# Order of the opening transfers, of the first feed-forward steps and of PE's instructions in an attention and feed-forward kernel

## The chip, the cores and the metric

The kernel runs on 1 core of one Trainium2 chip. The metric is device time in microseconds (us) of one execution. A core has five engines with a queue each: PE (matmuls and transposes), DVE and ACT (elementwise work and reductions), POOL (here only constants at the start) and SP, which issues all the DMA transfers of this kernel.

## The reference

Three stages in float32 (weights arrive as float64 and are converted on the chip):

```
attention: q, k, v are (2 batches, 8 heads, 768 positions, 64)
  k_sum = max of k over blocks of 32,  v_sum = mean of v over blocks of 32   (24 blocks)
  scores = q.k / 8 where |i - j| < 16 (else -1e9), beside q.k_sum / 8 + log(32)
  out = softmax(scores over both parts) @ [v, v_sum]
x = out as (1536 tokens, 512)
x = relu(x @ w_in)^2 @ w_out                         (d_ff 2048)
x = x / rms(x) * g;  out = (silu(x @ w_gate) * (x @ w_val)) @ w_out2   (d_ff 1536)
```

## The kernel before

**Attention** goes by groups of 128 queries of all 8 heads: 12 groups, 6 per batch. For a batch, `prep_load` loads the keys in three chunks, `prep_k` transposes a chunk on PE, takes the block maxima on DVE and copies the transposed keys to `kT` on ACT, and `prep_kend` puts the maxima between them. `vm_load` and `vmean` make the block means of the values (tile `vm`, evacuated by ACT at L383), and `vmfix` copies them by four small transfers per call into the tile `vx`, next to the value rows that `vload(g)` (six transfers, L404) puts there for a group. `vx` holds two groups at a time. A group is then `qload`/`qprep` (queries of two groups: load, transpose, scale), `scores` (PE, L418), `softmax` (DVE and ACT), `ptrans` (transposes on PE, copies to `pT` on ACT, L468), and `av` (PE, L488, needs `pT` and `vx`), whose result `split_xs` parts into a high and a low half `xhi`, `xlo`. `softmax` has two ways of taking the exponential: with `EXPACT(g)` true eight activations on ACT, one per head, that also sum; otherwise one long activation, with the subtraction and the sum as two more passes on DVE (L452, L454).

**Feed-forward 1** goes in three rounds over d_ff (4, 6 and 6 blocks of 128: `ROUNDS1`). The first round is woven into the attention: the loop over `k_` (six steps) takes two groups of tokens per step, with `h_pair(k_, f)` (x @ w_in, 24 matmuls of 128x256) and `y_pair(k_, f)` (12 matmuls of 128x512 into `y`) for f = 0 and 2, and between them the attention of the groups `g = 2 k_ + 3` and `g + 1`. Rounds 2 and 3 and feed-forward 2 follow, a stream of dense matmuls. Every product is three matmuls (high x high, high x low, low x high).

**Weights** come as 512 KB tiles of raw float64 (L160 for `wi`, L164 for `wo`). The class `Units` takes them in the list `order` (`wi0..3`, `wo0..3`, then those of round 2, ...) through four stages: `load`, `conv_a` (two activations on ACT, L175 and L176), `conv_b` (four passes on DVE, L182 to L189) and `split` (ACT L195, DVE L196). `tick()` moves one tile on by one stage in each of them; `until(u)` ticks until `u` is ready; `TICKS` extra ticks stand at the end of a step of the first round. `cap` holds loads to eight tiles until the third step. Raw tiles, converted tiles and the loaded keys, queries and value chunks share one tag of 14 tiles (`NW`).

**What sets the order.** The kernel text gives a program order. When it is compiled, a scheduler walks a modelled timeline and puts on each engine's queue what is ready first there, earlier program order winning; so each engine's order, SP's too, can differ from the text. Waits between the engines are added after that. `tc.manual_schedule` holds the engines that it names to program order. `tc.issue_after`, wrapped by `after(mark)`, puts all that is issued in its block behind the marked instruction on the same engine's queue, without waiting for its end.

**The opening of the text before:** keys of batch 0, queries 0, weight tiles `wi0`, `wi1` (`E0`), queries of the groups 2 and 3, values, weight tiles up to the sixth (`E1`), `prep_k`, scores 0, row loads `vload(0)` and `vload(1)`, scores 1, `vmean`, `vmfix`, and then groups 2, 3 and 4 with `av(0)` to `av(2)`; the loop over `k_` begins with the keys of batch 1.

Of the kernel before, what the change touches and what calls it, by code (L numbers as in the profile page):

```python
# [32 lines left out]
def tile_window_attention_moe_moe2(  # L33
# [13 lines left out]
    nc = tc.nc  # L47
# [19 lines left out]
    NG = NT // P  # L67
    NC2 = GPB // 2
# [164 lines left out]
                self.tick()  # L233

    def EXPACT(g):
        return g < 2 or g % 2 == 1

    def PARTS(g):
        return 2 if g < 3 else 1

    QB = 2
    E0, E1, TICKS = 2, 6, 2
    WARM = 10
    WOLAG = 2
    order = [("wi", f) for f in range(ROUNDS1[0])] + [("wo", f) for f in range(ROUNDS1[0])]
# [9 lines left out]
    units1 = Units(order)  # L255
# [18 lines left out]
    mark = {}  # L274
# [34 lines left out]
    def prep_begin(b):  # L309
        ksum = ap_.tile([P, NPAIR, NB], F32, tag="ksum", name=f"ksum{b}", bufs=1)  # L310
        state[b] = ksum
# [28 lines left out]
    def prep_kend(b, a):  # L340
        ksum = state[b]
        gaps = kT[:, :, WIN : WIN + NW1 * STEP].rearrange("d p (n s) -> d p n s", s=2 * STEP)
        half = ksum[:, :, GAP * a : GAP * (a + 1)]
        nc.vector.tensor_copy(
            gaps[:, :, :, STEP * a : STEP * a + GAP],
            half.unsqueeze(2).to_broadcast([P, NPAIR, NW1 // 2, GAP]),
        )
        if a == 0:
            nc.vector.tensor_copy(kT[:, :, WIN + NW1 * STEP : WIN + NW1 * STEP + GAP], half)
# [4 lines left out]
    def qload(g):  # L354
        b, r = divmod(g, GPB)
        state[("q", g)] = token_chunk(q, b, r // 2, f"qr{g}")
# [30 lines left out]
    def vmfix(i0, n):  # L387

        vt = vx.rearrange("k (i u) h d -> k u i (h d)", u=2)
        for u in range(2):  # L390
            for j, a in ((WIN, u), (K0 + QT, 1 - u)):
                rows = state["vm"][GAP * a : GAP * (a + 1)]
                nc.sync.dma_start(  # L393
                    vt[j : j + GAP, u, i0 : i0 + n], rows.unsqueeze(1).to_broadcast([GAP, n, DM])
                )

    def vload(g):
        b, r = divmod(g, GPB)
        i0 = 2 * g % NVX
        for u in range(2):  # L400
            t0 = r * P + u * QT
            for j, n, o in ((0, WIN, t0 - WIN), (K0, QT, t0), (K1, WIN, t0 + QT)):
                o = min(max(o, 0), S - n)
                nc.sync.dma_start(  # L404
                    vx[j : j + n, i0 + u], v[b, :, o : o + n, :].rearrange("h s d -> s h d")
                )
# [19 lines left out]
    def softmax(g):  # L426
        r = g % GPB
        mk = masks["first" if r == 0 else ("last" if r == GPB - 1 else "mid")]
        sl = state.pop(("s", g))
        te = ap_.tile([P, 2, NPAIR, NK], F32, tag="t", name=f"t{g}", bufs=TB)  # L430
        t = te.rearrange("q e p n -> q (e p) n")
        state[("t", g)] = t
        mx = ap_.tile([P, H], F32, tag="mx", name=f"mx{g}", bufs=TB)
        sm = ap_.tile([P, H], F32, tag="sm", name=f"sm{g}", bufs=TB)
        parts = PARTS(g)
        n = H // parts
        for i in range(parts):
            hs = slice(n * i, n * i + n)
            tv, m_, s_ = t[:, hs], mx[:, hs], sm[:, hs]
            for e in range(2 // parts * i, 2 // parts * (i + 1)):  # L440
                nc.vector.tensor_tensor(  # L441
                    te[:, e], sl[e], mk.unsqueeze(1).to_broadcast([P, NPAIR, NK]), op=ALU.add
                )
            if EXPACT(g):
                nc.vector.reduce_max(m_, tv, axis=AX.X, negate=True)
                for h in range(hs.start, hs.stop):
                    mark[("exp", g)] = nc.scalar.activation(
                        t[:, h], t[:, h], AF.Exp, bias=mx[:, h : h + 1], accum_out=sm[:, h : h + 1]
                    )
            else:  # L450
                nc.vector.reduce_max(m_, tv, axis=AX.X)
                nc.vector.tensor_tensor(tv, tv, m_.unsqueeze(2).to_broadcast([P, n, NK]), op=ALU.subtract)  # L452
                mark[("exp", g)] = nc.scalar.activation(tv, tv, AF.Exp)
                nc.vector.reduce_sum(s_, tv, axis=AX.X)  # L454
            nc.vector.tensor_scalar_add(s_, s_, 1e-9)
            nc.vector.reciprocal(s_, s_)
            mark[("norm", g)] = nc.vector.tensor_tensor(
                tv, tv, s_.unsqueeze(2).to_broadcast([P, n, NK]), op=ALU.mult
            )
# [21 lines left out]
    def av(g):  # L481
        pT = state.pop(("pT", g))
        ps = psA(f"xps1_{g}")
        for u in range(2):
            for p in range(NPAIR):
                o = p * P + QT * u
                for e in range(2):
                    nc.tensor.matmul(  # L488
                        ps[QT * e : QT * e + QT, o : o + QT],
                        vx[:, (2 * g + u) % NVX, 2 * p + e, :],  # L490
                        pT[:, e * NPAIR + p, QT * u : QT * u + QT],
                        start=True, stop=True,
                    )
        split_xs(ps, g, 1)
        state["done"] = g
# [85 lines left out]
    def group(g):  # L581

        scores(g)
        if g > 3:
            vload(g)
        softmax(g)
        if g + 2 < NG and g % 2 == 0:
            qload(g + 2)


    wz = cpool.tile([P, P], F32, name="wz")
    nc.vector.memset(wz, 0.0)
    nc.scalar.activation(ss[:, 0:1], wz[:, 0:1], AF.Exp)
# [4 lines left out]
    for c in range(NC2):  # L598
        prep_load(0, c)
    qload(0)  # L600
    units1.load(E0)
    qload(2)
    for c in range(NC2):
        vm_load(0, c)
    units1.load(E1)
    for j in (0, LK - WIN):
        nc.gpsimd.memset(kT[:, :, j : j + WIN], 0.0)
    prep_k(0, 0)
# [4 lines left out]
    qprep(0)  # L613
    prep_kend(0, 1)
    scores(0)
    vload(0)
    vload(1)
    softmax(0)
    scores(1)
    for c in range(NC2):  # L620
        vmean(0, c)
    vmfix(0, NVX // 2)
    softmax(1)
    rot["tags"] = ("a", "x")
    units1.ahead = 3
    qprep(2)
    ptrans(0)
    group(2)
# [5 lines left out]
    vload(3)  # L634
    ptrans(2)
    qprep(4)
    av(2)
    group(4)


    def steps_of(rounds, firsts):
# [31 lines left out]
        t = square(ps, f"0_{k_}_{f}")  # L673
        hq[(k_, f)] = hsplit(t, CH, f"0_{k_}_{f}")

    def y_pair(k_, f):
        if f == 0:
            for m in range(2):
                ys[m] = y_tile(k_, m, "y0_")
        hh = hq.pop((k_, f))  # L680
        for j in range(2):
            units1.until(("wo", f + j))
            ff_out(
                [ys[m] for m in range(2)], [t[:, G2 * j : G2 * (j + 1)] for t in hh],
                W[("wo", f + j)], f + j == 0, f + j == ROUNDS1[0] - 1,
            )
        if k_ == NK2 - 1:
            units1.used += 4
        if f == ROUNDS1[0] - 2:
            for m in range(2):  # L690
                gather(2 * k_ + m, ys.pop(m), 0, ROUNDS1, "y", None)

    def keys(b):
        prep_begin(b)
        for c in range(NC2):
            prep_k(b, c)
        prep_kend(b, 0)
        prep_kend(b, 1)

    for k_ in range(NK2):
        g, last = 2 * k_ + 3, 2 * k_ + 3 >= NG
        if k_ == 0:
            for c in range(NC2):
                prep_load(1, c)
        h_pair(k_, 0)
        if not last:
            ptrans(g)
        if g == GPB - 1:  # L710
            group(GPB)
        h_pair(k_, 2)
        if not last:
            av(g)
        if g == GPB - 1:
            for c in range(NC2):
                vmean(1, c)
            vmfix(0, 1)
        if g + 2 < NG:
            group(g + 2)  # L720
            if g + 2 == GPB + 1:
                vmfix(1, 1)
        y_pair(k_, 0)
        if g + 1 < NG:
            ptrans(g + 1)
        if k_ == 0:
            keys(1)
            for c in range(NC2):
                vm_load(1, c)
        elif g + 3 < NG:  # L730
            qprep(g + 3)
        y_pair(k_, 2)
        if g + 1 < NG:
            av(g + 1)
        if k_ == 0:
            qprep(GPB)
        elif g + 3 < NG:
            group(g + 3)
        if k_ == 2:
            units1.cap = NW - 3  # L740
        for _ in range(TICKS):
            units1.tick()
        if not last and g == NG - 1:
            actx.close()
            rot["tags"] = ("a",)
            side["pool"] = ctx.enter_context(
                tc.tile_pool(name="w2pool", bufs=1, side="right", reuse_waits="tile")
            )
            side["psum"] = ctx.enter_context(
                tc.tile_pool(name="psY2", bufs=1, space=PSUM, reuse_waits="tile")  # L750
            )
            grow = side["pool"].tile([P, DM], F32, tag="grow", name="grow")
            nc.sync.dma_start(grow, rms_g.partition_broadcast(P))
            units1.cap = NW + NRIGHT - 3

    steps1 = [s_ for s_ in steps_of(ROUNDS1, FIRST1) if s_[0] > 0]
    n1 = len(steps1)
    for i in range(n1 + 2):
# [97 lines left out]
```

## Time and profile before

| what | value |
|---|---|
| median of 3 runs (lowest, highest) | 694.28 us (691.59, 694.9) |
| the profiled execution | 692.37 us, its span 690.7 us |
| PE busy | 655.9 us, 95% of the span |
| DVE, ACT, POOL busy | 409.0, 300.6, 4.1 us |
| mean granted clock of PE | 0.97 of full |
| bytes read from HBM | 50.07 MB |
| transfers under 512 B a packet | 46080 of 78188 packets |

The span runs from the first to the last instruction; what the profiled execution has beyond it (1.7 us) lies outside. The shares are averages over the whole span, and the kernel has stages with different limits, so they don't say what bounds a stage. A clock of 1.00 is 2.4 GHz, 0.50 is 1.2 GHz. Idle time of PE is listed in the profile with the event that ended it.

### The profile page before, as it was taken

To read this page: it belongs to the slowest core of one execution; us is meant where nothing else is said; L and a number is where in the kernel's file an instruction comes from. 1 tells how busy PE (TensorE), PEld (TensorE's weight loads), DVE (VectorE), ACT (ScalarE), POOL (GpSimd) and SP (SyncE) were. 2 spreads that over 40 slices of the span, in tenths; PEclk is the share of its full clock that TensorE was granted. 3 is DMA by queue.
4 is the path that set the end of the run, shared out by engine and by line. 5 is a ranking of instruction groups with operands and counts; after the bars stand their busy time and mean duration, and the time that the engine had idled before them with its cause. 6 is when DMAs were issued, how large, how long until landed. Compare 5 with 4: busy or idle time off the path is not lost.

```text
span 690.7 us, 9362 instructions
## 1 busy us (share of the span) xinstructions
PE 655.9 (95%) x3644; PEld 532.7 (77%) x3644; DVE 409.0 (59%) x737; ACT 300.6 (44%) x607; POOL 4.1 (1%) x25
## 2 busy tenths in 40 slices
PE   6838998799999999999999999999999999999997
PEld 5337867688888888888888888888888888888885
DVE  4976858784999838924856596269933131313132
ACT  4835646655675526525453664257621121111110
POOL 2000000000000000000000000000000000000000
PEclk9758999899999999999999999999999999999999
DMA  9994244341722222101023043014300000001011
GB/s 232 276 236 115 47 115 121 94 126 26 248 88 85 81 79 93 61 1 49 13 70 113 31 143 101 1 61 123 121 1 1 0 1 0 1 0 62 1 61 62
DMA packets 78188, 54.22 MB, mean 79 GB/s; under 512 B 46080, under 2 KB 72704, under 8 KB 78144
## 3 DMA queue, kind: packets, MB, share of 16 engines
q1 hardware_dynamic: 78144, 53.62, 26.7%
q8 instruction: 29, 0.48, 0.3%
q14 instruction: 15, 0.12, 0.1%
HBM read 50.07 MB, written 3.15 MB: 77 GB/s over the span
## 4 chain that ended last, share of the span: by engine, by line
PE 84%; DVE 6%; DMA 4%; SPq 3%; ACT 2%; issue 1%; DVEq 0%; ACTq 0%
PE h L509 19%; PE y L530 18%; PE g L509 14%; PE v L509 14%; PE z L530 14%; DMA raw_wi<-in_moe_w_in_dram 2%; PE xps L488 2%; DMA raw_wo<-in_moe_w_out_dram 1%; PE s L418 1%; SPq L404 1%; DVE t L441 1%; SPq L303 1%; PE xps L500 1%; SPq L393 1%; DMA vx<-in_v_dram 1%
## 5 line engine op out<-in xcount | busy, mean ns | idle before, releaser
L509 PE MATMUL h<-xhi,w_wi 128*128 128x512 f32 (+1 forms) x480 | 132.8, 350 | 2.1 <-DMA vx<-in_v_dram 2.1
L530 PE MATMUL y<-w_wo,hhi 128*128 128x512 f32 x384 | 121.3, 399 | 0.0
L802 DVE TENSOR_TENSOR sg<-v,sg 128x512 f32<-128x512 f32 x36 | 24.8, 690 | 134.8 <-PE v L509 134.8
L509 PEld LDWEIGHTS h<-xhi,w_wi 128*128 128x128 f32 x480 | 84.8, 189 | 15.0 <-ACT xhi L478 2.3
L509 PE MATMUL v<-xhi,w_wv 128*128 128x512 f32 x288 | 95.5, 392 | 0.0
L509 PE MATMUL g<-xhi,w_wg 128*128 128x512 f32 x288 | 95.3, 392 | 0.0
L530 PE MATMUL z<-w_wp,hhiz 128*128 128x512 f32 x288 | 89.3, 393 | 0.0
L509 PE MATMUL h<-xlo,w_wi 128*128 128x512 f32 (+1 forms) x240 | 83.8, 350 | 0.9 <-DVE xlo L479 0.9
L530 PEld LDWEIGHTS y<-w_wo,hhi 128*128 128x128 f32 x384 | 71.8, 189 | 16.0 <-ACT u_wi L176 0.3
L530 PE MATMUL y<-w_wo,hlo 128*128 128x512 f32 x192 | 74.8, 395 | 0.0
L800 ACT ACTIVATE sg<-g 128x512 f32<-128x512 f32 x36 | 21.5, 598 | 103.9 <-PE g L509 101.6
L509 PEld LDWEIGHTS g<-xhi,w_wg 128*128 128x128 f32 x288 | 54.0, 188 | 12.3
L509 PEld LDWEIGHTS v<-xhi,w_wv 128*128 128x128 f32 x288 | 54.0, 188 | 12.1
L530 PEld LDWEIGHTS z<-w_wp,hhiz 128*128 128x128 f32 x288 | 54.0, 188 | 12.1
L658 ACT ACTIVATE r<-h 128x512 f32<-128x512 f32 x48 | 28.7, 598 | 69.8 <-PE h L509 69.7
L509 PE MATMUL g<-xlo,w_wg 128*128 128x512 f32 x144 | 56.6, 393 | 0.0
L509 PE MATMUL v<-xlo,w_wv 128*128 128x512 f32 x144 | 56.5, 392 | 0.0
L530 PE MATMUL z<-w_wp,hloz 128*128 128x512 f32 x144 | 56.0, 393 | 0.0
L659 DVE TENSOR_TENSOR r<-h,r 128x512 f32<-128x512 f32 x48 | 33.0, 687 | 36.3 <-ACT r L658 35.9
L520 ACT CAST hhiz<-sg 128x512 fp32r<-128x512 f32 x36 | 22.3, 620 | 70.6 <-DVE sg L802 70.3
L509 PEld LDWEIGHTS h<-xlo,w_wi 128*128 128x128 f32 x240 | 45.4, 189 | 7.4 <-DVE xlo L479 1.1
L530 PEld LDWEIGHTS y<-w_wo,hlo 128*128 128x128 f32 x192 | 35.8, 188 | 8.1
(125 smaller groups left out, 900.5 us busy)
## 6 DMA issues: line engine op xcount, KB each, us to landing
raw_wi<-in_moe_w_in_dram SPq DMA_DIRECT2D x16, 512.0 KB
raw_wo<-in_moe_w_out_dram SPq DMA_DIRECT2D x16, 512.0 KB
raw_wg<-in_moe_w_gate_dram SPq DMA_DIRECT2D x12, 512.0 KB
raw_wv<-in_moe_w_val_dram SPq DMA_DIRECT2D x12, 512.0 KB
raw_wp<-in_moe_w_out_dram SPq DMA_DIRECT2D x12, 512.0 KB
kr<-in_k_dram SPq DMA_DIRECT2D x12, 256.0 KB
qr<-in_q_dram SPq DMA_DIRECT2D x12, 256.0 KB
vr<-in_v_dram SPq DMA_DIRECT2D x6, 512.0 KB
```

The source lines that it names most:

```text
L303: nc.sync.dma_start(t[:, j].rearrange("p (h d) -> p h d", h=H), src[b, :, o : o + P, :].rearrange("h p d -> p h d"),)
L393: nc.sync.dma_start(vt[j : j + GAP, u, i0 : i0 + n], rows.unsqueeze(1).to_broadcast([GAP, n, DM]))
L404: nc.sync.dma_start(vx[j : j + n, i0 + u], v[b, :, o : o + n, :].rearrange("h s d -> s h d"))
L418: mark[("s", g)] = nc.tensor.matmul(sl[e][QT * u : QT * u + QT, p, :], qT[rr, p, QT * u : QT * u + QT], kT[rr, p, o : o + NK], start=True, ...
L488: nc.tensor.matmul(ps[QT * e : QT * e + QT, o : o + QT], vx[:, (2 * g + u) % NVX, 2 * p + e, :], pT[:, e * NPAIR + p, QT * u : QT * u + QT ...
L509: nc.tensor.matmul(ps, a_, b_, start=(i == 0), stop=(i == tot - 1))
L520: nc.scalar.copy(hi[:, 0:n], s[:, 0:n])
L530: nc.tensor.matmul(y, a_[:, ms], b_, start=(first and i == 0), stop=(last and i == 2))
L658: nc.scalar.activation(t, ps, AF.Relu)
L659: nc.vector.tensor_tensor(t, ps, t, op=ALU.mult)
L800: nc.scalar.activation(t, psg, AF.Silu)
L802: nc.vector.tensor_tensor(t, psv, t, op=ALU.mult)
```

## The change

Seven edits in one. (1) The exponential of the groups 1, 5 and 9 goes the long way over DVE instead of that of 2, 4, 6, 8 and 10. (2) The extra ticks of the six steps are 0, 0, 1, 1, 2, 3 instead of 2 each. (3) Only `wi0` is loaded early; the next seven weight tiles are put on SP's queue behind the last transfer of `vmfix`. (4) The row loads `vload(0)` and `vload(1)` come ahead of the second load of queries. (5) `av(2)` and group 4 move from the opening into the first step, behind `h_pair(0, 0)`, so that the feed-forward begins when two groups are done. (6) In the first step the three chunks of batch 1's keys are transposed before and inside `y_pair(0, 2)` rather than all before it. (7) From the start to the end of the first round PE takes its instructions in program order.

```diff
     def EXPACT(g):
-        return g < 2 or g % 2 == 1
+        return g % 4 != 1
...
-    E0, E1, TICKS = 2, 6, 2
+    TICKS = (0, 0, 1, 1, 2, 3)
...
-                nc.sync.dma_start(
+                mark["vmfix"] = nc.sync.dma_start(
...
+    hand = ExitStack()
+    hand.enter_context(tc.manual_schedule(engines={mybir.EngineType.PE}))
     wz = cpool.tile([P, P], F32, name="wz")
...
     qload(0)
-    units1.load(E0)
-    qload(2)
+    units1.load(1)
     for c in range(NC2):
         vm_load(0, c)
-    units1.load(E1)
+    vload(0)
+    vload(1)
+    qload(2)
...
     scores(0)
-    vload(0)
-    vload(1)
     softmax(0)
     scores(1)
     for c in range(NC2):
         vmean(0, c)
     vmfix(0, NVX // 2)
+    with after("vmfix"):
+        units1.load(8)
     softmax(1)
...
     qprep(4)
-    av(2)
-    group(4)
...
-    def y_pair(k_, f):
+    def y_pair(k_, f, between=()):
...
+            if between:
+                between[j]()
...
         h_pair(k_, 0)
+        if k_ == 0:
+            av(2)
+            group(4)
         if not last:
             ptrans(g)
...
         if k_ == 0:
-            keys(1)
+            prep_begin(1)
+            prep_k(1, 0)
+            y_pair(k_, 2, (lambda: prep_k(1, 1), lambda: prep_k(1, 2)))
+            prep_kend(1, 0)
+            prep_kend(1, 1)
             for c in range(NC2):
                 vm_load(1, c)
-        elif g + 3 < NG:
-            qprep(g + 3)
-        y_pair(k_, 2)
+        else:
+            if g + 3 < NG:
+                qprep(g + 3)
+            y_pair(k_, 2)
...
-        for _ in range(TICKS):
+        for _ in range(TICKS[k_]):
             units1.tick()
...
+    hand.close()
     steps1 = [s_ for s_ in steps_of(ROUNDS1, FIRST1) if s_[0] > 0]
```

## Rows read from the trace of the kernel before

**Rows 1.** The page's slices: 40 equal parts of the span, in tenths.
```profile
PE   6838998799999999999999999999999999999997
PEclk9758999899999999999999999999999999999999
```
**Rows 2.** Stretches: length, busy time (x instructions) by engine, PE's clock, DMA share, GB/s.
```profile
20.00:30.00 10.00, 9.41 (x39) 3.35 (x37) 9.88 (x27) 10.00 (x40) 0.00 (x0) 0.78 1.00 301
36.80:46.90 10.10, 0.00 (x0) 0.01 (x1) 6.61 (x15) 2.68 (x5) 0.00 (x0) 0.50 0.96 227
46.90:58.40 11.50, 8.96 (x96) 7.68 (x96) 7.59 (x15) 6.74 (x24) 0.00 (x0) 0.64 0.90 246
58.40:105.00 46.60, 46.42 (x468) 37.07 (x468) 32.66 (x52) 24.55 (x54) 0.00 (x0) 0.96 0.32 72
105.00:130.00 25.00, 18.53 (x195) 15.84 (x196) 20.10 (x35) 16.24 (x40) 0.00 (x0) 0.87 0.34 103
130.00:178.00 48.00, 46.93 (x463) 41.33 (x462) 34.73 (x59) 27.73 (x70) 0.00 (x0) 1.00 0.35 93
178.00:680.00 502.00, 502.00 (x2206) 409.80 (x2206) 277.70 (x502) 198.33 (x352) 0.00 (x0) 1.00 0.18 56
```
**Rows 3.** Waits of PE before 178 us: total us, times, longest us.
```profile
PE xps L488 <- DMA vx<-vm: 10.9, 2, 10.1
PE xps L488 <- ACT pT L468: 4.5, 1, 4.5
```
**Rows 4.** Timeline of SP, 0 to 60 us: start, length, what, count.
```profile
7.76 1.82 SPq L160 DMA_DIRECT2D raw_wi<-in_moe_w_in_dram  x2
...
16.81 2.24 SPq L160 DMA_DIRECT2D raw_wi<-in_moe_w_in_dram  x2
19.10 1.42 SPq L164 DMA_DIRECT2D raw_wo<-in_moe_w_out_dram  x2
20.56 10.17 SPq L404 DMA_DIRECT2D vx<-in_v_dram  x12
...
33.95 6.36 SPq L303 DMA_DIRECT2D kr<-in_k_dram  x6
40.42 1.41 SPq L164 DMA_DIRECT2D raw_wo<-in_moe_w_out_dram  x1
41.94 3.48 SPq L393 DMA_DIRECT2D vx<-vm  x4
45.52 0.45 SPq L164 DMA_DIRECT2D raw_wo<-in_moe_w_out_dram  x1
```
**Rows 5.** Timeline of PE: the first instructions of av(0) and av(2).
```profile
46.92 1.12 PE L488 MATMUL xps<-pT,vx 120*64 120x64 f32 x16 [10.14 <-DMA vx<-vm]
...
60.43 1.86 PE L488 MATMUL xps<-pT,vx 120*64 120x64 f32 x30
```
**Rows 6.** Timeline of ACT, 28 to 34 us: split of wi2, copy of means, split of wi3.
```profile
29.38 0.61 ACT L195 CAST w_wi<-x_wi 128x512 fp32r<-128x512 f32 x1
...
30.46 0.56 ACT L383 COPY vm<-vmean 24x512 f32<-24x512 f32 x1
...
32.99 0.61 ACT L195 CAST w_wi<-x_wi 128x512 fp32r<-128x512 f32 x1
```
**Rows 7.** Timeline of ACT, 117 to 126 us: the wait for a raw tile.
```profile
122.65 0.66 ACT L175 ACTIVATE x_wo<-raw_wo 128x512 f32<-128x512 f32 x1 [4.57 <-DMA raw_wo<-in_moe_w_out_dram]
```
**Rows 8.** The chain that ended last, around 136 us: start, length, what.
```profile
135.79 5.53 PE h L509 x46
```
**Rows 9.** Stretches, instructions on x_wo alone: length, DVE, ACT, clock, DMA, GB/s.
```profile
46.00:53.00 7.00, 4.46 (x8) 1.35 (x2) 0.50 0.90 250
60.50:62.50 2.00, 0.69 (x1) 0.61 (x1) 0.62 0.04 8
```
**Rows 10.** Stretches, instructions on t alone, columns as in rows 2 without POOL: groups 3, 4.
```profile
49.50:59.60 10.10, 1.41 (x8) 1.17 (x8) 3.61 (x4) 3.13 (x16) 0.67 0.80 200
63.40:71.60 8.20, 1.04 (x8) 0.89 (x8) 5.83 (x6) 1.01 (x1) 1.00 0.20 44
```

More of the change, by code (lines that the diff above doesn't have):

```diff
@@ L622, in tile_window_attention_moe_moe2 @@
     vmfix(0, NVX // 2)
+    with after("vmfix"):
+        units1.load(8)
     softmax(1)
     rot["tags"] = ("a", "x")
-    units1.ahead = 3
     qprep(2)
@@ L691, in y_pair @@
                 gather(2 * k_ + m, ys.pop(m), 0, ROUNDS1, "y", None)
[L693 to L698, printed above, removed]
     for k_ in range(NK2):
```

## The prediction, made blind

> **What bounds the kernel now.** I read the slices of the page first: PE is busy nearly everywhere except around 35 to 60 us and around 125 us, and its granted clock drops at the same places [rows 1]. The table of stretches puts numbers on that. From 178 us on PE is busy all the time at full clock: nothing there changes, and nothing can be won. From 36.8 to 46.9 us PE does nothing at all, the clock is at its lower level, and the DMA engines are 96% busy. From 105 to 130 us PE works 18.5 of 25 us [rows 2]. PE's own waits name the two long idle stretches: 10.1 us for `vx<-vm` (the block means that `vmfix` copies into the values' tile, wanted by `av(0)`), and 4.5 us for a `pT` copy on ACT [rows 3].
>
> Why are the means late? SP's timeline answers: their four transfers start at 41.94 us, behind six weight tiles (L160, L164) issued before 20.56, the row loads of `vx`, the batch-1 keys (6.36 us) and one more `wo` tile (1.41 us) [rows 4]. `av(0)` starts at 46.92, 1.5 us after the last of the four was issued at 45.42 [rows 4, 5]. The means themselves were ready at about 31.0 us on ACT [rows 6]. So the first bound is the order of SP's queue, behind DMA engines that have no room left. The second is ACT: at 117 to 122 us it waits 4.57 us for a raw `wo` tile, and the `pT` copy that PE wants is behind that [rows 7].
>
> **How much work is left.** Take `av(2)` as the mark; in the profile it runs from 60.43 [rows 5]. Busy time by granted clock from 58.4 to 178 is 46.4 x 0.96 + 18.5 x 0.87 + 46.9 = 107.6 us at full clock; about 1 us of it lies before 60.43 (2 us at the lower level). So 106.6 us of PE work took 178 - 60.4 = 117.6 us: **11 us were lost** after the mark, some 9 of them in the stretch 105 to 130 (25 less 16.1) [rows 2]. After the change, `h_pair(0, 0)` stands before the mark. It is 24 matmuls; 46 such took 5.53 us, so it is 2.9 us [rows 8].
>
> With T the new start of `av(2)` and L the new loss, the gain is (60.4 - T) + 2.9 + (11 - L).
>
> **Part by part: SP's order gives T.** Ahead of the means, SP loses `wi1` (half of 1.82 us), `wi2` and `wi3` (2.24), `wo0` and `wo1` (1.42): 4.6 us, all now held behind `vmfix` by the issue-order edge. The last `vx` row load was issued at 30.73, so SP is there at 26.2, `qload(2)` included, which only changes places with `vload(0)` and `vload(1)` [rows 4].
>
> What of the second group's queries and batch 1's keys, which nothing holds back? Loads and converted weights share one tag of 14 tiles. Before, the load of `wo2` follows `split(wi2)` in program order and that of `wo3` follows `split(wi3)`. On ACT the split of `wi2` (29.38) stands before the copy of the means (30.46) and that of `wi3` (32.99) after it; on SP `wo2` stands before the means' transfers and `wo3` after [rows 4, 6]. That is what tiles given out in program order look like. The queries and keys come after the seven weight tiles in the program, so I take it that they queue behind them, and behind the means.
>
> When the means are ready is not shown for the new order. Between 22 us (the values landed and PE free sooner) and the 31 us of now, I take 27: the copy now stands behind weight conversions on ACT [rows 6], most of which move away, and SP arrives at 26.2. Four transfers take 3.5 us and `av(0)` follows 1.5 us later: **32 us instead of 46.9**. `qload(2)` now lands at about that time too, so `scores(2)` may cost PE 1 us; it hides under the same wait.
>
> Then seven weight tiles (3.67 MB) at the 301 GB/s that 20 to 30 us shows: 12.2 us; the query tile and the keys, eight transfers of 262 KB, at 227 GB/s: 9.2 us [rows 2]; and `vload(2)`, which waits for `av(0)` and so queues last, 1.5 us more as the means did. 30.5 + 12.2 + 9.2 + 1.5 gives **T = 53.4**. Counted by SP's issue times it is earlier (30.5, weights 5.0, queries 2.1, keys 6.4, half of 10.17 for `vload(2)`, 1.5: 50.6), so the bytes decide. If `vload(2)` overtakes the keys, 1.57 MB drop out and T is 46.5.
>
> Do 3.67 MB right behind four small transfers hold those back? A `wo` tile was issued 0.1 us behind the means, and `av(0)` still began 1.5 us after them [rows 4, 5], so I count nothing for it. The Trainium skill ("DMA: Bandwidth & Descriptors", Queues, rings and completion order) has a rule that speaks against this order: descriptors carry no barrier, and a later one may finish its write before an earlier one. By that rule the weights could share the engines with the means; the row does not bear it out, and it is a rival below.
>
> **Conversions, on DVE.** A tile costs DVE 4.46/2 + 0.69 = 2.9 us [rows 9]. Before, six were done by 43 us, while PE waited; now one is, and 20.4 us of seven follow from 32 us on. With them go softmaxes 2 to 4 (3.61 us each [rows 10], and `xlo`, a pass like the 0.69 of [rows 9]: 12.9 us), squares and splits of two pairs (four such passes, 2.8) and three maxima of keys (2.1): 38 us, 39 with the short operations between, so `wo3` is ready at about 71. PE, unhindered, reaches `wo3` in `y_pair(0, 2)` four fifths of a step after T; a step is 106.6/6 = 17.8 us, so at 67.6. So **4 us of new loss**: PE, held in program order, can't step past it. If DVE's order puts weights first, it is 0.
>
> **TICKS.** At steps 0 and 1 ticks did nothing, since loads are capped at eight tiles. At step 2 the second tick converted a tile just ordered; this is the ACT wait that held `pT` up. With one tick the conversion comes a step later. I count the 4.5 us wait and the clock after it as gone (about 7.5 of the 9 us lost there [rows 2, 3]); at worst none goes.
>
> **EXPACT.** Groups 1, 5, 9 take the two extra DVE passes instead of 2, 4, 6, 8, 10: per group 2.2 us of DVE against 2.1 of ACT [rows 10]. Two groups fewer in all, so DVE has 4.4 us less and ACT 4.2 more over 120 us, with ACT busy 53 to 65% there [rows 2]: zero on the path. If ACT's cover were gone it is 4 us.
>
> **PE in program order, keys spread.** The same matmuls, so no work is added. Between `scores(g)` and `ptrans(g)` lie two thirds of a step by the program, some 12 us of other PE work; an ACT softmax takes 3.6 on DVE and 3.1 on ACT [rows 10], about 7 us in a row. That covers it with 5 us to spare. POOL's queue is not touched.
>
> **Sum.** L = 4 (late weights) + 2 (lower clock after the wait at T) + 2 (short waits as now [rows 3]) = 8. Gain 7.0 + 2.9 + 3 = 12.9 us. The profiled execution took 692.37 us, 1.9 below the median of the runs shown; 692.4 - 12.9 = 679.5, **679 us**.
>
> **Rivals.**
> - *Everything fits:* `vload(2)` gets in before the keys (T = 46.5) and DVE does weights first, so L = 3.5. 13.9 + 2.9 + 7.5 = 24.3 us: **668**. For it: a step asks DVE for only 13 to 15 of 17.8 us (two softmaxes with `xlo`, 4.3 to 6.5 each [rows 10], squares and splits 2.8, one copy 0.7, short operations about 1). Against: six transfers of keys are free to go as soon as the weights are out.
> - *Queries and keys take the free tiles and go before the means.* If tiles are not given out in program order, only 6.0 us leave SP's queue ahead of `vmfix` (`wo2` too): 36 instead of 42, `av(0)` at 41. T is then set by the weights, still about 53, but conversions begin at 43 and reach `wo3` some 6 us later: gain 7, **685**. For it: five of 14 tiles are free from the start, and keys need nothing else.
> - *The weights hold the means back.* If the means land only with the seven tiles, `av(0)` starts 12 us later, at 44, and T is 57.5 (`av(0)` to `av(2)` is 13.5 us in the profile [rows 5]): **683**. For it: the transfers share the same engines, which are full [rows 2]. Against it: the tile behind the means at 45.52 [rows 4]. This is where the skill's rule above leads.
> - *Slower: DVE's queue runs late in every step and PE pays it each time.* Now PE fills a wait with other matmuls; in program order `ptrans` waits at the head of its queue. In the steps 1 to 5 DVE has those 13 to 15 us of work in 17.8, and 2.9 more for each tile that a tick converts. The cover is 5 us; a softmax that comes 9 us behind stalls PE for 4, five times: 20 us, less the 12.9, **699**. It decides from 2.6 us a step (12.9/5). Against it: DVE is busy 70% from 58 to 105 us and PE hardly waits there [rows 2].
> - *It doesn't do what it says:* the means' copy stays late on ACT and `av(0)` stays near 45. Then T moves little and the new loss eats the rest: 690 to 694.
>
> **Chances.** The forecast 0.49, everything fits 0.20, keys first 0.13, means held back 0.03, slower 0.11, nothing happens 0.04. A measurement here tells about 0.5%, 3.5 us. Faster: 0.47 + 0.20 + 0.11 + 0.03 = 0.81; same: 0.02 + 0.02 + 0.03 = 0.07; slower 0.12 with a little of the last rival. The range takes in 668 and 685, with the bounds of T and of the loss around them (T 46.5 and L = 1: 60.4 - 46.5 + 2.9 + 10 = 26.8, 666, and a few us below it if the keys' 9.2 us hide wholly; T 57.5 and L = 15, where TICKS saves nothing: 1.8, 691): 662 to 691.
>
> **What would show it.** Right: `vx<-vm` starts on SP before 30 us and before the raw `wi1`; keys and queries after the `wo` tiles; `av(2)` at 50 to 55 us; a PE wait of a few us in the first `y_pair(0, 2)`; no wait of several us for `pT` near 110; the first round ends at about 165 us, and 513 us follow as now. Wrong: keys on SP ahead of `vx<-vm`, PE waits for `t` (DVE) in each step, or a new long wait for `vx<-in_v_dram`.

## The result, and the profile after

The changed kernel takes **685.08 us** (median of 4 runs, 684.16 to 687.51), the kernel before, measured beside it, 694.59 (4 runs, 691.59 to 695.62): ratio **0.9876 [0.9836, 0.9915]**, 1.2% faster. The forecast was 679, its range 662 to 691. The profiled execution took 685.15 us, span 683.4; against the 692.37 of before that is 7.2 us, where 12.9 were forecast.

The page's slices of the kernel after, to be held against [rows 1]:

```profile
PE   7776897999999999999999999999999999999997
PEclk9878898999999999999999999999999999999999
```

The third slice, 3 tenths in [rows 1], is now at 7; the weakest is the fourth, 6 tenths (51 to 68 us). Stretches of the kernel after, columns as in [rows 2]:

```profile
49.60:61.20 11.60, 9.74 (x161) 8.93 (x160) 11.55 (x22) 8.64 (x17) 0.00 (x0) 0.85 0.88 199
61.20:80.00 18.80, 12.83 (x97) 10.95 (x89) 16.93 (x30) 10.11 (x29) 0.00 (x0) 0.82 0.54 140
80.00:98.00 18.00, 18.00 (x182) 12.89 (x181) 10.72 (x18) 10.41 (x30) 0.00 (x0) 1.00 0.60 153
98.00:125.00 27.00, 22.20 (x226) 19.48 (x226) 19.28 (x34) 18.11 (x54) 0.00 (x0) 0.87 0.50 140
125.00:170.60 45.60, 44.51 (x443) 39.73 (x442) 31.10 (x51) 27.17 (x71) 0.00 (x0) 1.00 0.25 66
```

The first round ends at 170.5 us instead of 178, and all of the gain is made before that point: 512.9 us follow, as forecast.

SP's timeline of the kernel after, which answers to [rows 4]:

```profile
22.66 1.06 SPq L303 DMA_DIRECT2D qr<-in_q_dram  x2
26.53 3.46 SPq L393 DMA_DIRECT2D vx<-vm  x4
30.03 1.61 SPq L160 DMA_DIRECT2D raw_wi<-in_moe_w_in_dram  x3
31.69 2.16 SPq L164 DMA_DIRECT2D raw_wo<-in_moe_w_out_dram  x4
33.95 5.30 SPq L303 DMA_DIRECT2D qr<-in_q_dram  x2
39.34 6.76 SPq L404 DMA_DIRECT2D vx<-in_v_dram  x6
46.15 0.43 SPq L303 DMA_DIRECT2D kr<-in_k_dram  x1
46.68 3.59 SPq L404 DMA_DIRECT2D vx<-in_v_dram  x6
50.31 4.57 SPq L303 DMA_DIRECT2D kr<-in_k_dram  x5
```

The means go out at 26.53, the seven weight tiles right behind them; the row loads of `vload(2)` (39.34) come ahead of the keys (46.15 and 50.31). SP itself is free for the means at 23.72 (22.66 + 1.06) and stands 2.8 us: it waits for their copy on ACT, which stands behind the exponential of `softmax(1)` on that queue (24.86 to 26.03):

```profile
25.94 0.56 ACT L383 COPY vm<-vmean 24x512 f32<-24x512 f32 x1
```

PE's timeline of the kernel after, the first instructions of `av(0)` and `av(2)`, for [rows 5], with the query transposes in front of `h_pair(0, 0)` and the scores of group 4:

```profile
30.91 0.69 PE L488 MATMUL xps<-pT,vx 120*64 120x64 f32 x16
...
43.94 2.12 PE L364 MATMUL qps<-ident,qr 128*128 128x128 f32 x8 [1.90 <-DMA qr<-in_q_dram]
...
49.64 1.15 PE L488 MATMUL xps<-pT,vx 120*64 120x64 f32 x32
50.72 1.05 PE L418 MATMUL s<-kT,qT 64*64 64x120 f32 x32
```

`av(0)` starts 16.0 us earlier, without a wait, and `av(2)` 10.8 us earlier. `av(2)` doesn't wait either: from 45.71 to 49.64 PE works on `h_pair(0, 0)` and goes straight on. What PE then waits for (24 to 180 us; columns as in [rows 3]):

```profile
PE pps L467 <- DVE t L457: 6.2, 2, 6.0
PE qps L364 <- DMA qr<-in_q_dram: 6.2, 2, 4.3
PE xps L488 <- ACT pT L468: 5.2, 5, 2.2
```

The 6.0 us are new. Two narrow stretches of the kernel after show them, and what follows:

```profile
64.30:70.27 5.97, 0.01 (x1) 0.04 (x1) 5.97 (x11) 2.27 (x4) 0.00 (x0) 0.81 0.76 202
70.27:74.00 3.73, 3.73 (x17) 3.73 (x18) 3.61 (x7) 1.25 (x3) 0.00 (x0) 0.50 0.11 32
```

PE stands still while DVE has no gap at all, and after the stop PE works 3.73 us at 1.2 GHz. This is what DVE does in that time, below the first addition of `softmax(4)` (timeline of DVE, kernel after):

```profile
55.88 1.22 DVE L441 TENSOR_TENSOR t<-s,mask_mid 128x480 f32<-128x480 f32 x2
...
64.29 0.17 DVE L455 TENSOR_SCALAR sm<-sm 128x8 f32<-128x8 f32 x1
64.36 1.15 DVE L451 TENSOR_REDUCE mx<-t 128x8 f32<-128x960 f32 x1
65.42 0.69 DVE L521 TENSOR_TENSOR hlo<-r,hhi 128x512 fp32r<-128x512 f32 x1
66.02 0.69 DVE L186 SCALAR_TENSOR_TENSOR x_wo<-raw_wo,x_wo 128x512 uint32<-128x512 uint32 x1
66.62 0.20 DVE L456 RECIPROCAL sm<-sm 128x8 f32<-128x8 f32 x1
66.74 0.64 DVE L196 TENSOR_TENSOR w_wo<-x_wo,w_wo 128x512 fp32r<-128x512 f32 x1
67.30 1.16 DVE L452 TENSOR_TENSOR t<-t,mx 128x960 f32<-128x960 f32 x1
68.36 0.69 DVE L189 CUSTOM_DVE_ANT_0 x_wo<-x_wo,u_wo 128x1024 uint16<-128x1024 uint16 x1
68.97 1.15 DVE L457 TENSOR_TENSOR t<-t,sm 128x960 f32<-128x960 f32 x1
...
71.10 0.68 DVE L196 TENSOR_TENSOR w_wo<-x_wo,w_wo 128x512 fp32r<-128x512 f32 x1
```

PE wants L457, the last pass of `softmax(4)`. That softmax needs only L455, L456 and L457 here, 1.5 us. Between them stand passes of `softmax(5)` (L451, L452), a low half and three weight passes. The last pass of `wo3` begins at 71.10.

**Where the gain went.** With `av(2)` as the mark, lost time is length less busy time by clock. After 49.6 us that is 3.3 + 8.3 + 0 + 7.7 + 1.1 = 20.4 us, 11 before. The mark came 10.8 us earlier. What moved ahead of it is seen in PE's instructions by line, up to the mark, in the kernel before and in the kernel after:

```profile
L509 PE MATMUL h<-xhi,w_wi 128*128 128x256 f32 x2 | 0.6, 422 | 2.1 <-DMA vx<-in_v_dram 2.1
...
L509 PE MATMUL h<-xhi,w_wi 128*128 128x256 f32 x16 | 4.0, 339 | 0.0
L509 PE MATMUL h<-xlo,w_wi 128*128 128x256 f32 x8 | 2.6, 324 | 0.0
```

That is 22 matmuls of `h_pair(0, 0)`, 2.6 us at the 5.53/46 us each of [rows 8]; of all other kinds both kernels have run the same number by then, within two. So T and moved work gave 13.4 instead of the forecast 9.9 us. The round ended 7.5 us earlier, so the loss took back 5.9 where 3 were to be gained, and L was some 17 us where 8 was forecast. The 20.4 of the sum by stretches is 3.5 us above that: busy time by clock counts the same matmuls at different length in different surroundings, so sums by stretch are good to a few us only.

### The profile page after: what moved, and what is told of

The parts are those of the page before. It is cut to its first block, busy times and chain, and to the rows that moved or that the text cites. A ratio compares the mean times of both kernels' runs of the same rounds, so it can differ in the third digit from the quotient of the medians.

```text
span 683.4 us, 9367 instructions
## 1 busy us (share of the span) xinstructions
PE 651.6 (95%) x3644; PEld 533.4 (78%) x3644; DVE 405.4 (59%) x733; ACT 305.1 (45%) x637; POOL 4.1 (1%) x25
## 4 chain that ended last, share of the span: by engine, by line
PE 82%; ACT 5%; DMA 4%; DVE 4%; SPq 4%; issue 1%; DVEq 0%; ACTq 0%
PE y L530 18%; PE h L509 17%; PE g L509 15%; PE v L509 15%; PE z L530 14%; ACT t L447 3%; DMA raw_wi<-in_moe_w_in_dram 2%; SPq L404 2%; DMA vr<-in_v_dram 1%; PE xps L488 1%; SPq L303 1%; PE pps L467 1%; SPq L393 1%; PE xps L500 1%; ACT pT L468 1%
## 5 line engine op out<-in xcount | busy, mean ns | idle before, releaser
L509 PE MATMUL h<-xhi,w_wi 128*128 128x512 f32 (+1 forms) x480 | 136.1, 358 | 0.0
L509 PEld LDWEIGHTS h<-xhi,w_wi 128*128 128x128 f32 x480 | 87.6, 196 | 12.9 <-issue 0.5
L509 PE MATMUL h<-xlo,w_wi 128*128 128x512 f32 (+1 forms) x240 | 85.4, 356 | 0.0
L509 PEld LDWEIGHTS h<-xlo,w_wi 128*128 128x128 f32 x240 | 47.2, 197 | 6.1
```

Of the source, the lines that this page charges most:

```text
L509: nc.tensor.matmul(ps, a_, b_, start=(i == 0), stop=(i == tot - 1))
```

## The experiments

The theory after the result: SP's order makes the gain, and three things take some of it back: conversions at 98 to 125 us, DVE's backlog at 60 to 70 us, and PE's program order. The rivals: only one of these, or the extra ticks and the exponential. The edits (5) and (6) were not run by themselves. The runs were made on several chips, where the kernel before took between 692.67 and 695.56 us; so kernels are compared by their ratios to the kernel before that was measured beside them.

**1. SP's order alone.** The kernel before with edits (3) and (4) and nothing else; PE free.

```diff
-    units1.load(E0)
-    qload(2)
+    units1.load(1)
...
-    units1.load(E1)
+    vload(0)
+    vload(1)
+    qload(2)
...
     vmfix(0, NVX // 2)
+    with after("vmfix"):
+        units1.load(8)
```

> The kernel before with parts 3 and 4 of the change alone: one weight tile early, the value rows ahead of the second queries, seven tiles behind the means' transfers; the opening with group 4, the ticks, the exponential and PE's free order as before. Theory 4 (SP's order is what brings the gain): the means go out at 26 to 28 us, 683 to 687 us. Rival (it needs the feed-forward to begin with two groups, since av(2) waits for its value rows until 50 us): 689 us or more.

Measured: 681.13 us, 0.9818 [0.9789, 0.9847]. That is below the 683 to 687 expected. SP's order by itself is worth 12.8 us against the 693.89 of the kernel before beside it, at least as much as all seven edits; the other five together bring nothing, and by these medians cost some 4 us (the two intervals still touch).

**2. Two more weight tiles early**, in the changed kernel, ahead of the means.

```diff
     qload(2)
+    units1.load(3)
```

> The changed kernel with the tiles wi1 and wi2 loaded behind the second queries, ahead of the means' transfers, where SP stands 2.7 us and the DMA engines are half busy. Theory 1: DVE gets up to 5.8 us of conversions before 32 us, the wait of 6.0 us shrinks by 3 to 6, 679 to 682 us. Rival (the start decides): the two tiles' 1.05 MB hold the means back by 3 us, av(0) begins at 34 instead of 31 and the time is 685 us or more.

Measured: 692.27 us, 0.9974 [0.9957, 0.999]; nearly the whole gain is gone. The means' transfers are issued at 32.40 instead of 26.53, `av(0)` starts at 36.18 and `av(2)` at 56.31. The cause is in the timeline of ACT:

```profile
29.34 0.66 ACT L175 ACTIVATE x_wi<-raw_wi 128x512 f32<-128x512 f32 x1 [3.90 <-DMA raw_wi<-in_moe_w_in_dram]
...
31.82 0.56 ACT L383 COPY vm<-vmean 24x512 f32<-24x512 f32 x1
```

and in one of its stretches:

```profile
30.50:33.00 2.50, 0.57 (x3) 0.57 (x4) 2.03 (x5) 2.37 (x6) 0.00 (x0) 0.86 0.00 0
```

The copy of the means (25.94 in the changed kernel) stands behind ACT's four activations on two weight tiles, and the first of these waits 3.90 us for its raw tile. Then nothing moves on the DMA engines at all (0 GB/s from 30.5 to 33). So weights that come early hurt in a second way, which the forecast touched only in passing: through ACT's queue, where the means wait for a weight tile that they don't need.

**3. PE left free in the changed kernel**, and **4. PE in program order in the kernel before.**

```diff
-    hand.enter_context(tc.manual_schedule(engines={mybir.EngineType.PE}))
```

> The changed kernel with PE's order left to the scheduler again. Theory 1 (the half of the gain that is missing went to DVE, which is full from 50 to 71 us with the conversions of seven weight tiles, so that PE has nothing to step over to): 685 us, within 3, and a PE wait of several us near 65 stays. Theory 2 (PE held in program order waits where it could do other matmuls): 679 us or less, and the 6.0 us wait for t in front of the pps of group 4 is gone.

Measured: 682.65 us, 0.9831 [0.979, 0.9873]. PE's wait for `t` falls from 6.0 to 2.5 us and the round ends at 165.2; in the median that is 2.4 us, inside the intervals. The result lies between the two theories: the order is part of that wait, not all of it.

```diff
+    hand = ExitStack()
+    hand.enter_context(tc.manual_schedule(engines={mybir.EngineType.PE}))
...
+    hand.close()
     steps1 = [s_ for s_ in steps_of(ROUNDS1, FIRST1) if s_[0] > 0]
```

> The kernel before with PE alone held in program order from the start to the end of the first round. Theory 1 (the order costs little): 694 us, within 4. Theory 2 (the order costs PE several waits): 699 us or more. If the order is what brings the gain: 688 us or less.

Measured: 698.74 us, 1.0074 [1.0047, 1.01], slower. PE's waits there:

```profile
PE xps L488 <- DMA vx<-vm: 14.3, 1, 14.3
PE pps L467 <- DVE t L457: 6.4, 1, 6.4
PE qps L364 <- ACT pT L468: 4.7, 1, 4.7
```

The wait for the means is longer than in [rows 3], and behind it stand waits of 6.4 and 4.7 us where the kernel before has one, of 4.5 us. The edit counted at zero costs 0.7% by itself.

**5. Two ticks a step**, and **6. the old choice of exponentials**, each in the changed kernel.

```diff
-    TICKS = (0, 0, 1, 1, 2, 3)
+    TICKS = (2, 2, 2, 2, 2, 2)
```

> The changed kernel with two ticks in every step, as before the change. The prediction's step (the smaller number of ticks takes the ACT wait for a raw tile away, some 7.5 us with the clock): 692 us. Theory 3 (the scheduler draws the conversions forward to about the same place whatever the step of the tick, since the stretch 98 to 125 us of the changed kernel loses 7.7 us and that of 105 to 130 us before lost 8.9): 685 us, within 2.

Measured: 684.23 us, 0.9865 [0.9822, 0.9909]: no difference.

```diff
-        return g % 4 != 1
+        return g < 2 or g % 2 == 1
```

> The changed kernel with the old choice of the exponential: groups 2, 4, 6, 8, 10 take two more passes on DVE, groups 1, 5, 9 two fewer. The prediction's step (no engine but PE is on the path there): 685 us, within 2. Theory 1 (DVE is the bound between 40 and 71 us): groups 2 and 4 add 2.2 us each in front of the pps that PE waits for, group 5 comes later: 687 to 690 us.

Measured: 685.71 us, 0.9885 [0.9848, 0.9922]: no difference.

**7. The ticks held in their place.** Why fewer ticks change nothing is seen in the changed kernel's ACT timeline:

```profile
98.12 0.67 ACT L175 ACTIVATE x_wi<-raw_wi 128x512 f32<-128x512 f32 x1 [2.13 <-DMA raw_wi<-in_moe_w_in_dram]
98.69 0.56 ACT L383 COPY vm<-vmean 24x512 f32<-24x512 f32 x1
...
102.60 0.67 ACT L176 ACTIVATE u_wo<-raw_wo 128x512 int32<-128x512 uint32 x1 [1.09 <-DVE x_wi L189]
103.17 1.05 ACT L468 COPY pT<-pps 120x512 f32<-120x512 f32 x2
```

The first passes over round 2's tiles still stand ahead of the means of batch 1 and of a `pT` copy, and wait there, the first for its raw tile (2.13 us), another for DVE (1.09 us). With two ticks a step (5) such a pass stands there too, at 97.48, ahead of the means' copy at 98.05. So the number of ticks doesn't set the place on the queue; that the scheduler takes the passes as soon as it finds them ready is what fits. So the tiles were tied to the last `pT` copy of their step:

```diff
-        for _ in range(TICKS[k_]):
-            units1.tick()
+        with after(("pT", min(g + 1, NG - 1))):
+            for _ in range(TICKS[k_]):
+                units1.tick()
```

> The changed kernel with the ticks of a step put behind the last pT copy of that step on ACT, so that the conversions of wi4, wi5, wi6 and wo4 can't be drawn forward to 85 to 112 us. Theory 3 (ACT's waits for raw tiles and DVE's passes on them make the 7.7 us loss from 98 to 125): half of it or more goes, 679 to 682 us. Rival (the loss comes of the second batch's means and the softmax in a row): 685 us, within 2, or more if the second round then waits for its first tiles.

Measured: 679.17 us, 0.9789 [0.9768, 0.9811], 0.9% below the changed kernel, with intervals apart. Two of its stretches:

```profile
61.20:80.00 18.80, 11.45 (x86) 9.87 (x84) 17.29 (x31) 9.56 (x25) 0.00 (x0) 0.82 0.51 132
...
98.00:125.00 27.00, 26.73 (x324) 23.38 (x323) 17.58 (x27) 17.09 (x52) 0.00 (x0) 1.00 0.20 48
```

From 98 to 125 us PE now works 26.73 of 27 us at full clock, and the 7.7 us lost there shrink to 0.3; the wait at 60 to 70 us is left (7.4 us). The Trainium skill ("PSUM — Partial Sum Buffer", Engine vs sequencer instructions) says that the queues of ScalarE (ACT) and VectorE (DVE) are strictly first in, first out; the traces agree: the means (98.69) and `pT` (103.17) stand behind an activation that waits (2.13 and 1.09 us).

**8. Less DVE work in the conversions.** In the changed kernel, three of the four DVE passes of `conv_b` (L183, L186, L189) are left out for `wo0` to `wo3`, so these weights are not the converted values.

```diff
-    def conv_b(raw, x, r):
+    def conv_b(raw, x, r, short=False):
...
+        if short:
+            return x
```

> The changed kernel, with three of the four DVE passes of conv_b (L183, L186, L189) left out for the tiles wo0 to wo3: 1.8 us of DVE less for each, 7.2 in all, in the stretch where DVE is full; nothing else is taken away. Theory 1 (DVE's conversions are what PE waits for): the 6.0 us wait in front of the pps of group 4 falls to 1 us or less, and with the clock behind it the time falls by 5 to 9 us, to 676 to 680. Theory 2 (the wait comes of PE's order): 684 us, the wait stays over 4 us.

Measured: 681.57 us, 0.9826 [0.98, 0.9852]. PE's longest wait for `t` is 3.8 instead of 6.0 us, the round ends at 167.3, the median is 3.5 us less, with intervals that still touch; both theories had named other numbers. DVE's conversions are part of that wait, not all of it.

**9. DVE's order.** With the ticks held, `softmax(5)`, its group and the conversions of `wo2` and `wo3` are put behind the last DVE pass of `softmax(4)`.

```diff
-                self.x[u] = conv_b(*self.a.pop(u))
+                with after(("norm", 4)) if u in (("wo", 2), ("wo", 3)) else ExitStack():
+                    self.x[u] = conv_b(*self.a.pop(u))
...
-            group(g + 2)
+            if k_ == 0:
+                with after(("norm", 4)):
+                    group(g + 2)
+            else:
+                group(g + 2)
```

> The changed kernel, PE in program order, with the pin, and besides with softmax(5), its group of probabilities and the conversions of wo2 and wo3 put behind the last DVE operation of softmax(4). Theory, DVE's order at 60 to 70 us holds ptrans(4) up: PE's wait for t there (7.4 us with the pin) falls under 2 us and the time to 673 to 675 us. Rival, DVE has too much to do there in any order: the wait moves on to softmax(5) or to the late wo tiles, 679 us again, PE then waiting for wo2 or wo3 or for the next t.

Measured: 682.78 us, 0.9822 [0.9795, 0.9849]: not better than the 0.9789 of 7. PE's waits of this kernel, and the stretch of the longest:

```profile
PE y L531 <- ACT w_wo L195: 6.5, 1, 6.5
...
PE pps L468 <- DVE t L458: 2.4, 2, 1.6
```

```profile
66.90:73.37 6.47, 0.01 (x1) 0.00 (x0) 6.47 (x10) 2.79 (x4) 0.00 (x0) 0.70 0.34 92
```

The long wait for `t` is gone (1.6 us are left), and a wait for a `wo` tile of about the same length has come, with DVE busy all through it (6.47 of 6.47). So it isn't the order on DVE: up to here DVE has some 6 us more to do than PE, held in program order, has other work to cover.

**10. PE free and the ticks held**, in the changed kernel (the edits of 3 and 7), and **11. the same with DVE's order of 9.**

> The changed kernel with PE left to the scheduler's own order and the ticks of a step held behind that step's last pT copy. Theory, the two losses are separate: the pin gave 6 us (679.2 against 685) and the freed PE 2.4 us (682.7 against 685), together 676 to 677 us, first round ending at about 163 us. Rival, both mend the same loss in the stretch 98 to 125 us: no better than the pin alone, 679 us.

Measured: **675.1 us**, 0.9719 [0.9688, 0.9751]. The two gains add up, and kernels 7 and 10, which differ in PE's order alone, stand apart by 0.7%.

> As the kernel before it, but with PE left to the scheduler's own order. Theory, order on DVE matters less when PE may step past a wait: within 2 us of the changed kernel with the pin and a free PE, 675 to 677 us. Rival, the two add: 671 to 673 us.

Measured: 674.8 us, 0.9713 [0.9681, 0.9744]: no difference to 10. Stretches of kernel 10:

```profile
61.20:80.00 18.80, 16.04 (x103) 14.18 (x99) 16.50 (x28) 10.19 (x24) 0.00 (x0) 0.91 0.46 123
...
125.00:170.60 45.60, 45.47 (x365) 39.09 (x365) 39.68 (x73) 35.13 (x85) 0.00 (x0) 1.00 0.54 171
```

**12. SP's order and held ticks on the kernel before**, with two ticks a step, the old opening and the old exponentials, PE free: the kernel of 1 with the edit of 7.

> The kernel before, with only SP's order of the change (one weight tile early, seven behind the means) and the ticks held behind the last pT copy of their step, still two to a step; PE free, old opening and old EXPACT. Theory, the pin mends a loss that the kernel before has too at 105 to 130 us: some 5 us below the 681.1 of SP's order alone, 675 to 677 us. Rival, with a free PE and the old opening the loss there is small already: 681 us, no change.

Measured: 682.08 us, 0.9816 [0.9783, 0.985]: no gain over 1. Three of its stretches:

```profile
98.00:125.00 27.00, 27.00 (x296) 24.08 (x295) 18.40 (x29) 17.66 (x53) 0.00 (x0) 1.00 0.18 42
125.00:170.60 45.60, 39.94 (x367) 34.23 (x364) 41.42 (x74) 31.48 (x67) 0.00 (x0) 0.93 0.53 168
...
164.00:172.00 8.00, 7.07 (x19) 5.59 (x20) 8.00 (x16) 6.10 (x11) 0.00 (x0) 0.57 0.87 301
```

Holding the tiles mends 98 to 125 us here too, but the time is lost again at the end of the round, where DVE is busy 8.00 of 8.00 us and PE runs near its lower clock. Kernel 10 has no such loss there. Which of its other differences (opening with the keys' place, ticks, exponentials) spares it that was not tried.

The lost time by stretch, each worked out as length less busy time by clock (us). The columns show where time is lost; they don't add up to the times (7 and 10 differ by 9.3 us in the table and by 4.0 in their spans, 677.6 and 673.6):

| kernel | 49.6-61.2 | 61.2-80 | 98-125 | 125-170.6 |
|---|---|---|---|---|
| the change | 3.3 | 8.3 | 7.7 | 1.1 |
| 7, ticks held | 1.7 | 9.4 | 0.3 | 2.5 |
| 10, ticks held, PE free | 0.3 | 4.2 | 0 | 0.1 |
| 1, SP's order alone | 0 | 3.5 | 3.5 | 2.5 |
| 12, with ticks held | 0.3 | 3.2 | 0 | 8.5 |

## Why the prediction was right, and where it was not

The direction and the range held; the forecast was 6 us too low. Step by step:

- **SP's order: right.** The means were to go out at 27 us and went at 26.53; `av(0)` was to start at 32 and started at 30.91. SP was to be there at 26.2; it was free at 23.72 and stood until the means' copy on ACT was done, so ACT and no longer SP sets that time. Experiment 1 shows that this edit carries the gain, experiment 2 that undoing a part of it gives the gain back.
- **Tiles given out in program order: right for the order of weights, queries and keys; wrong for T.** Queries and keys did queue behind the seven weight tiles, so "queries and keys first" is out; that the tag of tiles sets this order was not tried. But the keys did not stand ahead of `vload(2)`: it went out at 39.34, before them. T was 49.64, between the forecast 53.4 and the 46.5 named for that case, so the term 60.4 - T was 10.8 us instead of 7.0. Nor did the row loads set T: `av(2)` waited for nothing, and the last wait ahead of it was 1.90 us for queries, in front of `h_pair(0, 0)`. The moved work was about as forecast (2.6 us for 2.9).
- **Weights don't hold the means back: right.** The weights were issued 0.04 us behind the last of the means (29.99), and `av(0)` started 0.9 us after that without a wait, sooner than the 1.5 us of [rows 4, 5]. The Trainium skill's rule that descriptors carry no barrier ("DMA: Bandwidth & Descriptors", Queues, rings and completion order) costs nothing visible in this run.
- **Conversions on DVE: the backlog was right, its price too low.** `wo3` was to be ready at about 71 us; its last pass began at 71.10. PE stopped 6.0 us, not at the `wo` tile as forecast but at `ptrans(4)`, for the softmax whose passes stand between the weights'. With the lower clock after it the stretch lost 8.3 us, and the stretch before it 3.3; the sum had 4 for the late weights and 2 for the clock. Experiment 9 moved the stop to the `wo` tile, at about the same length; either way DVE is late.
- **TICKS: wrong.** The step counted about 7.5 us as gained, since "with one tick the conversion comes a step later". It didn't, and 98 to 125 us lost 7.7 us, nearly the 9 of before. The sign that was named for it held all the same: no wait of several us for `pT` came, the longest was 2.2. Experiment 5 shows that the number of ticks does nothing, experiment 7 that holding the tiles gives 0.9%, 6 us. This step alone is about as large as the whole miss.
- **PE in program order: wrong to count at zero.** "About 7 us in a row" for a softmax, with 5 to spare, took an empty DVE for granted. The cover came out as forecast: from the end of the scores of group 4 (51.77) to where PE ran out of other work (64.30) are 12.5 us. But the first addition of `softmax(4)` began only at 55.88, 4.1 us after the scores, and its last pass ended at 70.1, 14.2 us later: 18.3 us in all, and what that has over the cover is the stop of 6.0. The price of the order is 0.7% in the kernel before (4), and 0.7% between kernels 7 and 10. The slower rival named this mechanism, but it had PE pay in every step; the long wait for `t` came once, in the first.
- **EXPACT: right**, no difference that can be measured (6).
- The "wrong if" list: no long wait for `vx<-in_v_dram` came, and keys were not ahead of the means; a long PE wait for `t` came, but only in the first step.

So the sum missed by two terms of opposite sign: T and moved work came out 3.5 us better, L some 9 us worse (12.4 by the sum of the stretches). That the forecast lay within 6 us is in part luck: `vload(2)` went ahead of the keys, which the forecast had only as a rival's case, and the earlier T hid a part of the loss.

## What to carry to other kernels

Find what the first stalled engine waits for, and put that transfer ahead of the bulk loads; one such edit was worth all seven here. Fixing an engine to program order takes away its cover for late producers: price it by the elapsed time of the producer on its loaded engine, not by the sum of its passes. Moving prefetch work in the text doesn't move it on the queue if a scheduler takes whatever is ready; tie it behind the latency chain, and look at the end of the round, where the held work must still fit.

## What the runs showed that was not expected

Two 512 KB tiles loaded early delayed the means by 5.9 us (26.53 to 32.40) while the DMA engines stood at 0 GB/s for 2.5 us of it: the damage was an activation waiting at the head of ACT's queue. And a 5.97 us stop of PE was followed by 3.73 us of work at 1.2 GHz, so this wait cost more than its length: 8.3 us were lost in the stretch from 61.2 to 80 us.
